# Head pairs stacked on 64x64 array tiles, the second dense product moved to the slot tiles, half of the expert weights loaded late

## The chip, the cores and the metric

The kernel runs on one core of one Trainium2 chip. The metric is the device time of one execution in microseconds; shown times are medians of several runs. A core has five engines with their own instruction queues: PE (matmuls; its weight loads are listed apart as PEld), DVE, ACT, POOL and SP. SP only issues transfers here; POOL computes and also issues the transfers that cast or that gather and scatter rows. Every transfer runs on the core's 16 DMA engines. SBUF is the on-chip memory, PSUM holds matmul results until DVE or ACT has read them (eight banks of 2 KB for each of 128 partitions).

## The reference

Attention with normalised q and k, then a mixture of experts with one expert for each token beside a dense layer that every token passes.

```python
# q, k, v: (8, 12, 448, 64) float32; x below: 3584 tokens of 768
def rmsnorm(x, g):
    return x / np.sqrt(np.mean(x * x, axis=-1, keepdims=True) + 1e-06) * g
scores = (1 / np.sqrt(64)) * np.matmul(rmsnorm(q, g_q), rmsnorm(k, g_k).transpose(0, 1, 3, 2))
attn = softmax(scores)                     # over the last axis
x = np.matmul(attn, v)                     # heads side by side: 12 * 64 = 768
y_dense = np.maximum(x @ w1_dense, 0.0) @ w2_dense          # 768 -> 512 -> 768
expert_idx = np.argmax(x @ w_gate, axis=1)                  # 8 experts
gate_w = softmax(x @ w_gate)[arange, expert_idx]
for e in range(8):                                          # 768 -> 512 -> 768
    y_moe[mask_e] = gate_w[mask_e] * (np.maximum(x[mask_e] @ w1[e], 0.0) @ w2[e])
out = y_dense + y_moe
```

## The kernel before

**Attention** goes in 48 steps `t`, one for two heads (a pair), six for a batch. The 448 positions of a head are spread as 112 partitions of `JJ` = 4. q and k come in groups `g` of two pairs (L141, on SP), v as bf16 (L145, on POOL). `squares` (L161 on POOL, L162 on DVE) and L167/L168 on ACT give 1/rms as `r`; `normalise` multiplies on DVE (L177); `transposes` brings q and k to 64 rows a head (L186) and copies them out on DVE (L191 with the gains, L193). `scores(t, j)` multiplies 64 rows of k by q for both heads (L202), each head in its half of the rows, and ACT takes the exp of 112 x 896 values (L204). `attend(t, hh)` multiplies the exps by v with a column of ones (L215, 16 matmuls), and DVE divides by the sum (L219, L221). `xtrans` transposes the result (L228, copied by ACT, L230); after six pairs `route(b)` makes the logits of a batch (L239), takes the best expert into `oh`, and SP writes x and the gate into a table `records` in HBM, one row for each token (L260 to L264).

The dense layer of the batch before runs in pieces between these: `dense1` (L273, relu on ACT, L276) and `dense2` (L284, copied by ACT and DVE, L289 and L291); SP writes the 768 results into the token's record (L293). The 16 expert weight blocks, 768 KB each in bf16, are cast on the way by transfers that POOL issues every 2.5 steps (L329) into `we`, which holds all experts.

In attention the order on PE, POOL and SP is the program's order, written by hand: in step `t` come scores of `t + 1`, transposes of `t + 2`, squares of `t + 4`, normalise of `t + 3`, attend of `t`, and pieces of the dense layer. DVE and ACT are ordered by the compiler. Four PSUM buffers (`wkp`) serve transposes, attend, dense and logits; two pairs of banks serve the scores.

**The slot table** (L357 to L442) follows when all batches are routed: for each token its place among the tokens of its expert, then a one-hot `sel` (L410) and `val` (L416), and 32 matmuls (L422) that give for each slot the record's `row` and the output row `dest`. A slot tile is 128 slots of one expert; there are 35.

**The slot tiles**: POOL gathers 128 records (L449), PE transposes x (L460), multiplies by the expert's w1 (L469, relu and gate on ACT, L474), transposes (L479, copied by ACT, L481) and multiplies by w2 (L487); DVE adds the dense result from the record (L493) and POOL scatters the rows to the output (L495).

## Time and profile before

| | |
|---|---|
| median of 3 runs | 518.86 us (514.01 to 518.98) |
| the profiled execution: time, span | 519.15 us, 517.3 us |
| busy: PE, DVE, ACT, POOL | 399.3, 326.6, 274.8, 205.3 us |
| granted PE clock, mean | 0.92 |
| HBM read, written | 83.16 MB, 31.20 MB |
| first scores | 27.4 us |
| last attend ends | 335.3 us |
| first gather is issued | 373.9 us |
| first transpose of a slot tile, last w2 matmul | 379.1 us, 510.1 us |

The profile page lists one profiled execution. In rows of groups, `out<-in` names the tiles, x is the count, then come busy us and mean ns of one instruction, then the idle time ahead and what ended it. Windows give the busy us of each engine in a stretch of the span, the granted clock of PE (1.00 is full), the share of time that the 16 DMA engines were busy, and GB/s. Timeline rows begin with start and length in us; an x above 1 means that many instructions merged into one row, and a length of matmuls reaches to the end of the last one's pipeline, so that the pace is read from start to start.

### The profile page before, as it was taken

Reading aid. Unit: us, or ns where it says so; the run is one execution under the profiler, and the core shown is the slowest. Engines: PE = TensorE matmul, PEld = TensorE weight load, DVE = VectorE, ACT = ScalarE, POOL = GpSimd, SP = SyncE. Lnnn points to the kernel's source line nnn. Section 1 sums busy time; section 2 is a strip of 40 time slices with the busy share of each in tenths; the row PEclk is TensorE's granted clock in tenths of the full one; section 3 lists DMA queues with packets and bytes.
Section 4 is the critical chain, followed back from the end, with each engine's and each line's share of the span. In section 5 each row is a group of like instructions: output and inputs, shape, how many; then the busy total and the mean of one; then the engine's idle time right before and its main releaser. Section 6 shows DMA issues by size and latency. Waiting matters only on the chain.

```text
span 517.3 us, 10774 instructions
## 1 busy us (share of the span) xinstructions
PE 399.3 (77%) x4010; PEld 232.7 (45%) x4010; DVE 326.6 (63%) x761; ACT 274.8 (53%) x431; POOL 205.3 (40%) x223
## 2 busy tenths in 40 slices
PE   0189888769688887788977979980249889899894
PEld 0046645435344454454543545650215555556552
DVE  3796999868568779588786975427603434444442
ACT  0077887648567756767855978730003333333331
POOL 6674354453426327128136130000023555556542
PEclk9999999979888989979977999996559999999998
DMA  8999679997798599959879441251063878888860
GB/s 142 237 218 175 151 154 159 192 256 96 176 269 137 137 271 142 198 133 239 187 134 248 107 144 30 81 152 46 1 241 122 278 253 266 286 283 266 294 259 2
DMA packets 66017, 92.62 MB, mean 179 GB/s; under 512 B 8749, under 2 KB 56109, under 8 KB 65968
## 3 DMA queue, kind: packets, MB, share of 16 engines
q0 software_dynamic: 31568, 52.48, 45.4%
q1 hardware_dynamic: 34400, 39.46, 27.6%
q8 instruction: 33, 0.54, 0.4%
q14 instruction: 16, 0.13, 0.1%
HBM read 83.16 MB, written 31.20 MB: 221 GB/s over the span
## 4 chain that ended last, share of the span: by engine, by line
PE 30%; DMA 27%; DVE 20%; ACT 7%; issue 6%; POOL 6%; SPq 2%; POOLq 0%; DVEq 0%; ACTq 0%
DMA xq<-in_q_dram 9%; DMA xg<-records,row 9%; DMA xk<-in_k_dram 8%; DVE y L177 7%; PE he L469 5%; PE av L215 5%; DVE ssq L162 5%; PE ps L202 5%; PE yp L487 4%; ACT ex L204 4%; POOL sq L161 4%; PE ff L273 4%; PE ff L284 2%; DVE xa L221 2%; PE tr L186 2%
## 5 line engine op out<-in xcount | busy, mean ns | idle before, releaser
L204 ACT ACTIVATE ex<-ps 112x896 bf16<-112x896 f32 x192 | 173.8, 921 | 54.3 <-PE ps L202 52.7
L161 POOL TENSOR_TENSOR sq<-xq 112x512 f32<-112x512 f32 x48 | 52.1, 1085 | 141.8 <-DMA xq<-in_q_dram 118.8
L162 DVE TENSOR_REDUCE ssq<-sq 112x8 f32<-112x512 f32 x96 | 64.0, 672 | 42.9 <-POOL sq L161 42.9
L202 PE MATMUL ps<-y 64*112 64x448 bf16 x384 | 84.1, 435 | 2.5 <-DVE y L193 1.3
L215 PE MATMUL av<-va,ex 112*128 112x65 bf16 x1536 | 71.2, 202 | 17.7 <-DVE xa L221 16.0
L215 PEld LDWEIGHTS <-ex 112*128 112x128 bf16 x1536 | 59.3, 103 | 40.9 <-DVE xa L221 21.3
L284 PE MATMUL ff<-wd,hT 128*112 128x384 bf16 x256 | 60.4, 347 | 10.8 <-DVE xa L221 10.8
L449 POOL DMA_INDIRECT xg<-records,row x35 | 33.9, 967 | 81.1 <-DVE dest L442 70.4
L186 PE MATMUL tr<-ident,y 112*128 112x112 bf16 x384 | 39.2, 232 | 29.0 <-DVE y L177 24.2
L161 POOL TENSOR_TENSOR sq<-xk 112x512 f32<-112x512 f32 x48 | 51.3, 1070 | 19.1 <-DVE ssq L162 9.8
L495 POOL DMA_INDIRECT out_dram<-ys,dest x35 | 35.6, 1018 | 58.6 <-DVE ys L493 58.6
L474 ACT ACTIVATE hs<-he,xg 128x512 bf16<-128x512 f32 x35 | 24.0, 687 | 65.6 <-DMA xg<-records,row 36.3
L469 PE MATMUL he<-we,xT 128*128 x210 | 53.5, 393 | 3.0 <-issue 1.5
L462 DVE COPY xT<-xp 128x768 bf16<-128x768 bf16 x35 | 19.5, 557 | 57.5 <-PE xp L460 57.5
L202 PEld LDWEIGHTS <-y 64*112 64x112 bf16 x384 | 26.2, 131 | 61.6 <-issue 56.0
L273 PE MATMUL ff<-xT,wd 128*128 128x448 bf16 x192 | 52.1, 373 | 2.1 <-DVE xa L221 2.1
L487 PE MATMUL yp<-we,heT 128*128 x280 | 51.2, 326 | 0.8 <-DVE ys L493 0.8
L493 DVE TENSOR_TENSOR ys<-yp,xg 128x768 f32<-128x768 f32 x35 | 33.5, 957 | 28.0 <-PE yp L487 28.0
L481 ACT COPY heT<-hp 128x512 bf16<-128x512 bf16 x35 | 20.5, 586 | 49.1 <-PE hp L479 49.1
L186 PEld LDWEIGHTS <-y 112*128 112x128 bf16 x384 | 22.9, 104 | 51.0 <-DVE y L177 25.3
L177 DVE TENSOR_TENSOR y<-xq,r 112x512 bf16<-112x512 f32 x48 | 45.0, 937 | 0.9 <-ACT r L168 0.9
L221 DVE TENSOR_TENSOR xa<-av,inv 128x256 bf16<-128x256 f32 x96 | 40.1, 418 | 1.4
(98 smaller groups left out, 473.3 us busy)
## 6 DMA issues: line engine op xcount, KB each, us to landing
we<-in_moe_w_dram POOLq DMA_DIRECT2D x16, 768.0 KB, 8.4
records<-ys SPq DMA_DIRECT2D x32, 336.0 KB, 3.3
xq<-in_q_dram SPq DMA_DIRECT2D x23, 448.0 KB, 6.7
xk<-in_k_dram SPq DMA_DIRECT2D x23, 448.0 KB, 7.0
vr<-in_v_dram POOLq DMA_DIRECT2D x24, 224.0 KB, 5.9
records<-xa SPq DMA_DIRECT2D x8, 576.0 KB, 7.4
wd<-in_moe_w_dense_dram POOLq DMA_DIRECT2D x2, 768.0 KB, 19.4
records<-xa SPq DMA_DIRECT2D x8, 96.0 KB, 7.0
```

The source lines that it names most:

```text
L161: nc.gpsimd.tensor_mul(sq, x, x)
L162: nc.vector.tensor_reduce(ssqs[g][:, n, 2 * i * JJ:(2 * i + 2) * JJ], sq.rearrange("p h (j d) -> p (h j) d", d=D), AX.X, ALU.add)
L177: nc.vector.tensor_mul(y.rearrange("p j h d -> p h j d"), x.rearrange("p h (j d) -> p h j d", d=D), rs[g][:, n, 2 * i * JJ:(2 * i + 2) * J ...
L186: nc.tensor.transpose(ps[:, j * SC:(j + 1) * SC], xn[name, t][:, j].rearrange("p h d -> p (h d)"), ident[:SC, :SC])
L202: nc.tensor.matmul(ps[:, hh, :S], qkT["k", t][d0:d0 + D, j * SC:(j + 1) * SC], qkT["q", t][d0:d0 + D, :], start=True, stop=True)
L204: nc.scalar.activation(exs[t][:, j], ps[:, :, :S], AF.Exp, scale=scale)
L215: nc.tensor.matmul(av[:, mi], exs[t][:, j, hh, QC[mi]:QC[mi] + P], vas[t // GP][:, 2 * (t % GP) + hh, j, :De], start=(j == 0), stop=(j == ...
L221: nc.vector.tensor_mul(xnats[b][:, :, h * D:(h + 1) * D], av[:, :, :D], inv.to_broadcast([P, 4, D]))
L273: nc.tensor.matmul(ffs[0], wd1[:, kk, ff * P:(ff + 1) * P], xTs[b][:, kk], start=(kk == 0), stop=(kk == KD - 1))
L284: nc.tensor.matmul(ffs[0], hTs[b][:, ff, j * SC:(j + 1) * SC], wd2[:, ff, dd * Dm // 2:(dd + 1) * Dm // 2], start=(ff == 0), stop=(ff == F ...
L469: nc.tensor.matmul(he, xTs[t][:, kk], we[:, bass.ds(eregs[t], 1), 0, kk * F:(kk + 1) * F] .rearrange("p o f -> p (o f)"), start=(kk == 0), ...
L487: nc.tensor.matmul(yp[:, dd, :HD], heTs[t][:, ff], we[:, bass.ds(eregs[t], 1), 1, ff * Dm + dd * HD:ff * Dm + (dd + 1) * HD] .rearrange("p ...
```

## The change

- Attention goes in 24 groups `g` of four heads. The 448 positions are spread as 64 partitions of `J` = 7, and two heads lie one above the other in the 128 partitions, `(r p)`. `scores(g, j)` is four matmuls of 64 rows by 64 columns, one for each quarter of the array, and one exp of 128 x 896; there are 7 of them in a group. `attend` multiplies 64 rows at a time, for the two stacked heads in turn: 112 matmuls a group; its two PSUM accumulators are filled over four calls.
- k is divided on POOL (q stays on DVE), v is copied on POOL, transposed k is copied out on ACT, transposed x on DVE.
- In a group, scores come in each of seven slots `i`, attend in the even ones, and full-array work (transposes, logits, ranks, dense) in the odd ones.
- Exps live in 14 buffers that are the last part of `we` (the space of experts 6 and 7 and the end of 5).
- Loads of q and k are called for group `g + 5` at the start of group `g`, in three buffers as before; one load fills 128 partitions with pieces of 1792 bytes instead of 1024.
- The dense layer's first product has tokens as rows; its relu, 512 values in bf16, is written to the record instead of the 768 results (a record has 704 instead of 1216 words). The second product is done in the slot tiles: each gathers the hidden values, transposes them (`hdTs`) and accumulates them with `wd2` into the same PSUM as the expert's product. DVE and ACT copy half of the sum each.
- Places within an expert and `sel` are made batch by batch (`ranks`); the slot table gives two values a slot instead of three, and every expert has at least one slot tile, so that tile `t` reads no expert above `t`.
- Of the 16 expert blocks eight are issued during attention, every 2.6 groups, and eight (experts 4 to 7) at the end of POOL's order in attention, ahead of the gathers.
- The gains are loaded from ACT's queue; constants are made after the first loads are issued.

```diff
-    JJ = 4
-    SC = S // JJ
+    J = 7
...
+    LATE, WPACE = 8, 2.6
...
+        xflat = we.rearrange("p e a f -> p (e a f)")[:, -NX * 2 * S:]
+        exr = [xflat[:, i * 2 * S:(i + 1) * 2 * S].rearrange("p (h s) -> p h s", h=2)
+               for i in range(NX)]
...
+                "(i r) (p j) d -> (r p) i (j d)", r=2, j=J)
...
+            nc.gpsimd.tensor_copy(vabs[g % 3][:, :, :, :D],
+                                  xin["v", g].rearrange("p h (j d) -> p h j d", d=D))
...
+        def squares(g, name):
+            x = xin[name, g]
+            ssq = sb.tile([P, 2, J], F32, tag="ssq" + name)
+            for hh in range(2):
+                sq = sb.tile([P, J * D], F32, tag="sq", bufs=3)
+                nc.gpsimd.tensor_mul(sq, x[:, hh], x[:, hh])
+                nc.vector.tensor_reduce(ssq[:, hh], sq.rearrange("p (j d) -> p j d", d=D), AX.X,
+                                        ALU.add)
+            r = sb.tile([P, 2, J], F32, tag="r" + name)
+            nc.scalar.activation(r, ssq, AF.Ln, bias=eps_t, scale=1.0 / D)
+            nc.scalar.activation(r, r, AF.Exp, scale=-0.5)
+            rs[name, g] = r
+
+        def normalise(g, name):
+            eng = nc.vector if name == "q" else nc.gpsimd
+            y = sb.tile([P, J, 2, D], BF16, tag="xn" + name, bufs=1)
+            for hh in range(2):
+                eng.tensor_mul(y[:, :, hh], xin[name, g][:, hh].rearrange("p (j d) -> p j d", d=D),
+                               rs[name, g][:, hh].unsqueeze(2).to_broadcast([P, J, D]))
+            xn[name, g] = y
...
             if name == "q":
-                nc.vector.tensor_scalar(y, ps, gqk, None, op0=ALU.mult)
+                nc.vector.tensor_scalar(o, i, gqk, None, op0=ALU.mult)
             else:
-                nc.vector.tensor_copy(y, ps)
-            qkT[name, t] = y
-
-        def scores(t, j):
-            if j == 0:
-                exs[t] = sb.tile([SC, JJ, 2, S], BF16, tag="ex", name="ex")
-            ps = scp.tile([SC, 2, 512], F32, tag="sc")
+                nc.scalar.copy(o, i)
...
+        def scores(g, j):
+
+            x = exr[(g * J + j) % NX]
+            exs[g, j] = x
+            qT, kT = qkT["q", g], qkT["k", g]
+            ps = scp.tile([P, 2, 512], F32, tag="sc", name="sc")
             for hh in range(2):
-                d0 = hh * D
-                nc.tensor.matmul(ps[:, hh, :S], qkT["k", t][d0:d0 + D, j * SC:(j + 1) * SC],
-                                 qkT["q", t][d0:d0 + D, :], start=True, stop=True)
-            nc.scalar.activation(exs[t][:, j], ps[:, :, :S], AF.Exp, scale=scale)
-
-        def attend(t, hh):
-
-            b, pr = divmod(t, NPR)
-            if pr == 0 and hh == 0:
-                xnats[b] = sb.tile([P, 4, Dm], BF16, tag="xa", name="xa")
+                rows = slice(hh * D, (hh + 1) * D)
+                for r in range(GP):
+                    nc.tensor.matmul(ps[r * D:(r + 1) * D, hh, :S], kT[rows, r, j],
+                                     qT[rows, r].rearrange("p j s -> p (j s)"),
+                                     start=True, stop=True)
+            nc.scalar.activation(x, ps[:, :, :S], AF.Exp, scale=scale)
...
+            va = vabs[g % 3]
+            if m == 0:
+                for r in range(GP):
+                    avs[r] = wkp.tile([P, 4, De], F32, tag="wk", name="av")
+            for j in range(J):
+                for r in range(GP):
+                    rows = slice(r * D, (r + 1) * D)
+                    nc.tensor.matmul(avs[r][:, m], exs[g, j][rows, hh, QC[m]:QC[m] + P],
+                                     va[rows, hh, j, :De], start=(j == 0), stop=(j == J - 1))
+            if m < 3:
+                return
+            for r in range(GP):
+                inv = sb.tile([P, 4, 1], F32, tag="inv")
+                nc.vector.reciprocal(inv, avs[r][:, :, D:])
+                h = 4 * gb + 2 * hh + r
+                nc.vector.tensor_mul(xas[b][:, :, h * D:(h + 1) * D], avs[r][:, :, :D],
+                                     inv.to_broadcast([P, 4, D]))
...
+            nc.vector.tensor_copy(xTs[b][:, gb * GP:(gb + 1) * GP], ps)
...
+        def ranks(b):
+
+            rk = wkp.tile([P, 5, E], F32, tag="wk", name="rk")
+            mm = [(rk[:, :4], tri, oh[:, b])]
+            mm += [(rk[:, i:4], ones, oh[:, b, :4 - i]) for i in range(1, 4)]
+            mm += [(rk[:, 4:], ones, oh[:, b, m:m + 1]) for m in range(4)]
...
+            nc.vector.tensor_tensor(sel[:, b], iop.unsqueeze(1).to_broadcast([P, 4, P]),
+                                    lo[:, b].unsqueeze(2).to_broadcast([P, 4, P]), ALU.is_equal)
...
+        def dense(n):
+            b, n = divmod(n, 4 * KD)
+            m, kk = divmod(n, KD)
+            if kk == 0:
+                ff[0] = wkp.tile([P, F], F32, tag="wk", name="ff")
+            nc.tensor.matmul(ff[0], xTs[b][:, kk, QC[m]:QC[m] + P], wd1[:, kk],
+                             start=(kk == 0), stop=(kk == KD - 1))
+            if kk == KD - 1:
+                hd = sb.tile([P, F], BF16, tag="hd", bufs=1)
+                nc.scalar.activation(hd, ff[0], AF.Relu)
+                r0 = b * S + m * P
+                n = P if m < 3 else D
+                nc.sync.dma_start(rec[r0:r0 + n, XH:GO], hd[P - n:].bitcast(F32))
...
+                for g in range(3):
+                    for name in "qk":
+                        squares(g, name)
+                        normalise(g, name)
+                        if g < 2:
+                            transposes(g, name)
+                    if g < 2:
+                        values(g)
+                    load(g + 3)
+                load_v(1)
...
+                for g in range(NG + 1):
+                    b, gb = divmod(g, NB)
+                    if g % 2 == 0:
+                        load_v(g // 2 + 2)
+                    if g > 0:
+                        load(g + 5)
...
+                    for i in range(J):
+                        if g + 1 < NG:
+                            scores(g + 1, i)
+                        if g < NG and i % 2 == 0:
+                            for m in range(2):
+                                attend(g, i // 4, i % 4 + m)
+                        if i == 1:
+                            if g > 0:
+                                xtrans(g - 1)
+                            if g + 2 < NG:
+                                transposes(g + 2, "q")
+                        if i == 3 and gb == 0 and g > 0:
+                            logits(b - 1)
+                        elif i == 5 and g + 2 < NG:
+                            transposes(g + 2, "k")
+                        if i == 5 and gb == 0 and g > 0:
+                            ranks(b - 1)
+
+                        if i % 2 and i > 1 and g >= NB and (gb > 0 or i == 5):
+                            for _ in range(5):
+                                if nd < (b - 1) * 4 * KD + 4 * KD:
+                                    dense(nd)
+                                    nd += 1
+                        if g + 3 < NG:
+                            if i % 4 == 0:
+                                squares(g + 3, "qk"[i // 4])
+                            if i % 4 == 2:
+                                normalise(g + 3, "qk"[i // 4])
+                        if i == 4 and g + 2 < NG:
+                            values(g + 2)
+                while nd < 4 * KD * B:
+                    dense(nd)
+                    nd += 1
+                while nw < len(wjobs):
+                    nc.gpsimd.dma_start(*wjobs[nw])
+                    nw += 1
+
+        run({PE, POOL, SP})
...
+            hp = ps1.tile([P, FT, P], BF16, tag="tr")
+            for i in range(FT):
+                nc.tensor.transpose(hp[:, i], xb[:, Dm + i * P:Dm + (i + 1) * P], ident)
+            hdTs[t] = sb.tile([P, FT, P], BF16, tag="hdT", name="hdT")
+            nc.vector.tensor_copy(hdTs[t], hp)
...
-            eregs[t] = nc.tensor.value_load(tei[:, t:t + 1], min_val=0, max_val=E - 1)
+            eregs[t] = nc.tensor.value_load(tei[:, t:t + 1], min_val=0, max_val=min(t, E - 1))
...
+                    nc.tensor.matmul(yp[:, dd, :HD], hdTs[t][:, i],
+                                     wd2[:, i, dd * HD:(dd + 1) * HD],
+                                     start=(i == 0), stop=False)
...
-            nc.vector.tensor_add(ys, yp[:, :, :HD],
-                                 xgs[t][:, XH:GO].rearrange("p (a d) -> p a d", a=2))
+            nc.vector.tensor_copy(ys[:, 0], yp[:, 0, :HD])
+            nc.scalar.copy(ys[:, 1], yp[:, 1, :HD])
```

## The prediction

> **What bounds the kernel now.** I read the stages first (windows of the span), then the DMA queues, then single stretches of the timeline, last the chain that ended last. Busy times of a window stand in the order PE, weight load, DVE, ACT, POOL, then granted clock, DMA share, GB/s.
>
> ```profile
> 50.00:75.00 25.00, 22.79 (x306) 13.79 (x304) 23.25 (x60) 21.57 (x34) 9.27 (x9) 1.00 0.69 151
> 125.00:150.00 25.00, 19.41 (x230) 11.45 (x231) 16.17 (x46) 15.61 (x25) 5.56 (x6) 0.89 0.94 192
> 312.00:335.00 23.00, 23.00 (x286) 13.53 (x283) 11.28 (x31) 19.61 (x30) 0.00 (x0) 1.00 0.14 39
> 379.10:517.30 138.20, 118.14 (x840) 68.69 (x840) 53.02 (x70) 44.54 (x70) 65.54 (x66) 0.94 0.69 232
> ```
>
> In the middle of attention no engine is full, but the DMA share is 0.94 and the clock sags. Counted by the exps (four to a step), the same windows for L204 alone give the pace:
>
> ```profile
> 50.00:75.00 25.00, 17.75 (x20) 1.00 0.69 151
> 125.00:150.00 25.00, 12.28 (x15) 0.89 0.94 192
> 300.00:325.00 25.00, 14.73 (x17) 1.00 0.21 63
> ```
>
> 20 exps in 25 us are 5.0 us a step; from 100 to 300 us all windows together hold 119, so 6.7 us a step, 13.4 us for two steps (one group of four heads). The waits and queues say why:
>
> ```profile
> POOL sq L161 <- DMA xq<-in_q_dram: 118.8, 13, 12.1
> q0 software_dynamic: 31568, 52.48, 45.4%
> q1 hardware_dynamic: 34400, 39.46, 27.6%
> ```
>
> 27.6% of 517.3 is 143 us of full DMA for 39.46 MB: 3.6 us/MB. q0 has 235 us; the tile stage, all q0, takes 0.69 of its 138 us and a little before, so 98; the other 137 us are the v and weight casts, 19.4 MB written: 7.1 us/MB, 5.5 us for a 768 KB expert job. Attention thus carries 280 us of transfers, and waits for them. PE's own pace is read where no loads are left:
>
> ```profile
> 311.06 0.40 PE L202 MATMUL ps<-y 64*112 64x448 bf16 x2
> 311.39 0.56 PEld L215 LDWEIGHTS <-ex 112*128 112x128 bf16 x16 [0.20 <-issue]
> 311.88 0.13 PEld L273 LDWEIGHTS <-wd 128*128 128x128 bf16 x2
> 311.92 0.54 PE L273 MATMUL ff<-xT,wd 128*128 128x448 bf16 x2
> 312.39 0.13 PEld L202 LDWEIGHTS <-y 64*112 64x112 bf16 x2 [0.37 <-issue]
> ```
>
> From start to start: the score pair takes 0.33 us, less than twice the 0.19 that one dense matmul of 448 columns is given, so its two 64-row halves run together and in the rest PE starts nothing; some 0.09 is lost ahead of it too: 0.42 a call. Sixteen attend matmuls take 0.49: 31 ns each. The slot tiles run at PE's pace except for gathers:
>
> ```profile
> 452.29 1.46 PE L469 MATMUL he<-we,xT 128*128 x6
> 453.58 0.50 PE L460 MATMUL xp<-ident,xg 128*128 128x128 bf16 x6
> 453.92 1.46 PE L487 MATMUL yp<-we,heT 128*128 x8
> 455.21 0.39 PE L479 MATMUL hp<-ident,hs 128*128 128x128 bf16 x4
> 455.44 1.46 PE L469 MATMUL he<-we,xT 128*128 x6
> ```
>
> Starts differ by 1.29, 0.34, 1.29, 0.23: 3.15 us a tile. Between the last attend (335.3) and the first gather issue (373.94) lie 38.6 us, a third of it three rows:
>
> ```profile
> 360.83 4.34 DVE sel L410
> 365.16 3.58 DVE val L416
> 368.78 3.00 PE slp L422 x32
> ```
>
> **The slot tiles: +38 us, the surest term.** The second dense product moves here: 8 more matmuls of 384 columns (1.29) and 4 more transposes (0.23) make 3.15 + 1.52 = 4.67 us a tile, 163 for 35. I add 6 us from first landing to steady running (two transposes and a gemm1 that took 2.72 at half clock) and the 7 us from the last L487 to the end: 176 against 138. A gather now brings 2.8 KB a slot instead of 4.9, so a tile moves 0.75 MB instead of 1.02 in a longer time, and I cost the wait for gathers at nothing; ACT and DVE, with the halves of ys, stay under 2 us a tile.
>
> **Transfers in attention: 280 to 210 us.** Eight expert jobs leave (44), and hidden activations are stored as 3.7 MB instead of 11 MB of products (26). Over a stage of some 260 us this is a share of 0.8. Loads are also called two groups ahead instead of one, and the SP queue is no longer held by the L293 stores. I cost the wait for loads at nothing; what hides it is that slack. Without it a 7 us load per group would show in part.
>
> **One group of four heads, engine by engine.** PE: 7 score calls of four 64x64 matmuls. The pair's second matmul costs nearly nothing now (lower bound 0.42 a call); upper bounds are 0.61 if two go together and 0.99 if none do. Both halves of the pair already overlap, so I take 0.47: 3.3 us. Attend: 112 matmuls of 64 rows instead of 64 of 112 rows. Bounds are 25 ns (19 logits matmuls took 0.47) and 31; at 28 it is 3.1 us, where it was 2.0. Transposes 0.7, xtrans 0.45, first dense product 8.3 at 0.215 = 1.8, logits and ranks 0.3. PE: 9.65. The second dense product, 1.9 us a group, is gone from here.
>
> The row says that a load of 112 columns shows 123 ns against 98 for 128 columns, so the narrower load is the slower one. The Trainium skill's "TensorEngine Tiling (Array Packing)", Restrictions, says that column tiling switches fast weight load off; by "TensorE: Matmul & The Clock Gate", LDWEIGHTS, 64 columns would take 53 ns. Four of them in a row, unhidden, would add 0.16 a call, an estimate of 27 us in all and a time near 532; by the pair's row it is 0.05.
>
> DVE: four square sums 0.672 x 448/512 (2.4), q divided (1.6 by L177), q transposes out (0.9), four inv and xa (2.4), x transposes out, taken from ACT (0.8), logits and ranks (1.1): 9.1; it was 11.6. ACT: seven exps at 0.92 (6.5), k transposes out, taken from DVE (1.1), relu (0.9), r (1.1): 9.5. POOL: squares 3.8, k division 1.9 by the same two-input row, v copy between 0.6 (DVE's L152) and 1.9 (L161 scaled), taken as 1.2, issues 0.8: 7.7. So three engines lie within 6%.
>
> PE's order then waits for PSUM. Two av accumulators are held across three slots, a dense accumulator across two, and four wk buffers serve all. Where av of the last half is still being read, xt and tr follow one another through one buffer (a 0.8 us copy plus DVE's queue), and a new ff waits for the relu. What queues behind is everything on PE, scores first, then ACT's exps. Bounds: 0 (before kept 93 to 100% of its fullest engine) to 2.6 us; I take 1.6. A group takes 11.3 us where it took 13.4. All this is at full clock; the granted clock was 0.86 to 0.97 from 100 to 300 us, where PE waited most, and 1.00 from 50 to 75 and after 300, so I expect 1.00. At 0.9 the 9.65 would be 10.7, which is 23 us in all and lies within the rivals' span.
>
> **Attention's end.** First scores need two whole groups, q and k, with k divided on POOL: 32 us where it was 27.4, then 6 for seven exps: 38. Three groups without dense 9.5 each, nineteen at 11.3, the last two 10 and 7: 298 instead of 335.3, so -37.
>
> **From there to the gather: 38.6 to 18 us.** The dense product and ys stores end (10 us), scans and positions are done per batch, sel too. Left: transposes, logits, ranks 7; counts and hi 2.5; tl and two val products of 1120 elements, 2 to 4 by L413's 1.32; slp 3.0; row and issue 1.6.
>
> **Late weights: +6 us.** Three jobs are free about 19 us ahead of attention's end, two follow when the last group but one is attended, three more only at its end, because exps lie in their place. At 5.5 each they drain near 26 us after it, and the gathers, in the same queue, are issued at 18. No row shows a gather behind weights. Bounds: nothing, landing 5.1 us after issue as now, to all eight after attention's end, 44 us and 2 more. I take landing at 29, so 6 us over. By the Trainium skill's "DMA: Bandwidth & Descriptors", section "Two DMAs through the same engine are not ordered", descriptors of one queue of one DMA engine start in order, which would give the same 29; no row here shows it.
>
> **Sum.** 298 + 29 + 176 = 503, against 517.3. The profiled execution took 519.15 with 1.85 around its span; the median is 518.86. So **505**; beside the median that is 0.3 us less, within its spread (514.01 to 518.98). Each us on a group is 22 us; no gain is left at 11.9 us a group.
>
> **Rivals.** (1) PSUM handover decides: PE's order stalls 2.6 us a group or more. For it: DVE, ACT and PE are almost equally full and four buffers carry long tenants; against: the 312 to 335 window, full PE. From 11.9 us a group it is slower; at 12.5, 505 + 26 = 531. (2) The engines overlap as well as in the 50 to 75 window, 93%: 10.4 us a group, 485. Against it: the longer tenants. (3) Weights hold the gathers whole: landing at 46 instead of 29, 522. For it: POOL waits in order, and a first job that waits for exps delays all behind it.
>
> **How the numbers follow.** Forecast 0.55, rival 1 0.20, rival 2 0.17, rival 3 0.08. A measurement here tells about 1% from no change. The forecast's own range is 492 to 518; the range, 482 to 530, leaves out the ends of rivals 1 and 2. Faster: 0.50 of the forecast, all of rival 2 and a little of 3; the same: the rest of the forecast and most of 3.
>
> **What would show it.** Seven exps every 11.3 us; DMA share near 0.8 in attention and the POOL wait for xq gone; score calls start to start under 0.5 us; tiles at 4.67; first gather issue 18 us after the last attend and landing some 11 later. It is wrong if groups take over 12 us, if score calls take 0.6 or more, or if gathers land over 40 us after attention.

## The result, and the profile after

The changed kernel takes 558.42 us (median of 4 runs, 557.07 to 560.32) where the kernel before takes 518.25 (4 runs on the same chip): a ratio of 1.079, 95% interval 1.072 to 1.086. Slower by 8%; the prediction was 505. The profiled execution took 559.05, its span 557.4. By stages:

| stage | before | predicted | after |
|---|---|---|---|
| first exp starts (predicted: first scores) | 28.1 | 32 | 25.9 |
| a group of four heads (exps 3 to 21) | 13.45 | 11.3 | 14.38 |
| last attend ends | 335.3 | 298 | 349.5 |
| from there to the first gather issue | 38.7 | 18 | 27.4 |
| from the issue to the first xg transpose | 5.2 | 11 | 3.9 |
| from there to the end | 138.2 | 176 | 176.6 |

By spans the miss is 54.4 us (557.4 against 503), and 51.5 of it lie in attention. What is lost from there to the first gather (9.4 us) is mostly made up by the first transpose behind it (7.1). The windows of after show the three stages (busy time in the order PE, weight load, DVE, ACT, POOL, then granted clock, DMA share, GB/s):

```profile
25.90:349.50 323.60, 243.22 (x4240) 139.50 (x4236) 189.07 (x485) 196.93 (x312) 157.88 (x178) 0.78 0.58 131
349.50:376.00 26.50, 13.31 (x96) 8.07 (x95) 9.71 (x41) 3.81 (x7) 1.57 (x2) 0.70 0.66 141
384.00:557.40 173.40, 165.81 (x1240) 101.97 (x1238) 49.38 (x103) 58.08 (x105) 64.76 (x65) 0.97 0.39 130
```

In attention no engine is full, PE is busy for 75% of the time, the DMA share is 0.58 where 0.8 was predicted, and the granted clock is 0.78. So the shares point neither to transfers nor to the work of any one engine. The instructions themselves came out cheaper than predicted, as PE's timeline shows where the clock is full, and the slot tiles came out as predicted:

```profile
195.04 0.38 PE L226 MATMUL sc<-y 64*64 64x448 bf16 x4
195.36 0.62 PE L244 MATMUL av<-va,we 64*128 64x65 bf16 x28
195.90 0.38 PE L226 MATMUL sc<-y 64*64 64x448 bf16 x4
...
440.99 1.46 PE L507 MATMUL he<-we,xT 128*128 x6
...
445.67 1.46 PE L507 MATMUL he<-we,xT 128*128 x6
```

From start to start, four 64x64 score matmuls take 0.32 us, and 28 attend matmuls 0.54 us, 19 ns each. A tile is 445.67 - 440.99 = 4.68 us.

What PE, POOL and VectorE wait for in attention is in the lists of waits from 60 to 310 us (who <- for what: us in all, times, longest):

```profile
PE av L244 <- DVE xa L252: 31.8, 16, 3.8
PE tr L206 <- DVE xT L263: 10.1, 11, 2.4
PE rk L302 <- DVE oh L284: 6.4, 5, 2.4
PE ff L329 <- ACT y L214: 5.5, 7, 0.9
...
POOL y L198 <- PE tr L206: 100.2, 12, 9.9
...
DVE ssq L187 <- POOL sq L186: 42.0, 27, 6.9
```

PE waits for VectorE to empty the av accumulators (xa), VectorE stands at POOL's squares, and POOL stands at PE's transposes of k: a ring. One turn of it, from the timeline (start, duration, engine; in brackets the idle time before and who ended it):

```profile
130.09 1.83 POOL L198 TENSOR_TENSOR y<-xk,r 128x448 bf16<-128x448 f32 x2 [7.17 <-PE tr L206]
131.87 0.81 POOL L172 DMA_DIRECT2D xv<-in_v_dram  x1
132.71 1.83 POOL L186 TENSOR_TENSOR sq<-xq 128x448 f32<-128x448 f32 x2
...
133.68 0.62 DVE L187 TENSOR_REDUCE ssq<-sq 128x7 f32<-128x448 f32 x1 [6.82 <-POOL sq L186]
134.57 0.62 DVE L187 TENSOR_REDUCE ssq<-sq 128x7 f32<-128x448 f32 x1 [0.26 <-POOL sq L186]
135.10 0.24 DVE L250 RECIPROCAL inv<-av 128x4 f32<-128x4 f32 x2
...
135.79 0.95 PE L244 MATMUL av<-va,we 64*128 64x65 bf16 x27 [2.42 <-DVE xa L252]
```

The tile of the divided k (xn) has one buffer, so POOL may not divide the next k until PE has transposed the last one; everything behind it in POOL's order, a v load and the next squares, is late by those 7 us. VectorE's order has the square sums (L187) ahead of inv and xa (L250, L252), so it holds the av accumulators meanwhile, and PE stands for 2.42 us. What happens to the clock is in five windows of 3.41 us around that gap:

```profile
131.49:134.90 3.41, 1.89 (x40) 0.90 (x38) 0.95 (x2) 1.14 (x2) 3.39 (x5) 1.00 0.56 139
134.90:138.31 3.41, 2.44 (x39) 1.80 (x40) 2.26 (x8) 2.37 (x6) 2.28 (x3) 0.50 1.16 245
138.31:141.73 3.42, 2.79 (x44) 1.73 (x44) 2.42 (x6) 0.97 (x2) 0.00 (x0) 0.50 0.18 63
141.73:145.14 3.41, 3.41 (x39) 1.37 (x37) 0.79 (x4) 2.07 (x3) 0.00 (x0) 0.50 0.11 38
145.14:148.55 3.41, 3.34 (x73) 1.85 (x68) 0.00 (x0) 3.20 (x5) 2.25 (x3) 1.00 0.01 2
```

The clock is 1.00 or 0.50, and in this trace it changes only at the edges of such windows. PE is busy for 0.55 of the first one, and the clock falls. It is busy for 0.71 and 0.82 of the next two, at half clock, and only after a window that it fills does the clock return: a gap of 2.42 us is followed by 10.2 us at half clock.

The same cut through the profiles of all sixteen kernels of the table below, from 60 to 310 us, shows what goes ahead of a change. At full clock, all 92 windows in which PE was busy for at most half were followed by half clock, and none of the 323 with 0.78 or more; of the 351 between, 90 were. At half clock, 133 of 139 windows with 0.95 or more were followed by full clock, 55 of 90 from 0.85 to 0.95, and 1 of 158 below that. So in these traces the clock follows how much PE was busy, and once it has fallen, short waits are enough to keep it down.

The clock's record begins with its first return to full, at 39.3 us here. Ahead of that the views read 1.00, but a score call takes 0.59 us, as it does at 0.50 later, instead of 0.38; these windows are counted as half clock above.

At the end of attention, the chain that ended last goes through writes of hd, whose tile has one buffer:

```profile
336.49 5.38 DMA records<-hd
...
342.59 7.24 DMA records<-hd
...
350.55 5.19 DMA records<-hd
...
356.47 5.31 DMA records<-hd
...
366.02 1.70 DMA records<-hd
...
370.89 4.02 PE slp L447 x32
```

Alone a write takes 1.7 us; beside the late expert weights, 5 to 7.

### The profile page after: what moved, and what is told of

It is laid out like the page before. It is cut to its first block, busy times and chain, and to the rows that moved or that the text cites. A ratio compares the mean times of both kernels' runs of the same rounds, so it can differ in the third digit from the quotient of the medians.

```text
span 557.4 us, 14089 instructions
## 1 busy us (share of the span) xinstructions
PE 429.4 (77%) x5628; PEld 254.7 (46%) x5628; DVE 262.0 (47%) x723; ACT 263.9 (47%) x434; POOL 250.4 (45%) x285
## 4 chain that ended last, share of the span: by engine, by line
issue 29%; PE 23%; POOL 21%; DVE 15%; DMA 8%; ACT 2%; POOLq 1%; ACTq 0%; DVEq 0%
POOL sq L186 8%; POOL xg L485 6%; PE av L244 6%; PE sc L226 6%; PE ff L329 5%; DMA records<-hd 5%; PE tr L206 4%; POOL y L198 3%; POOL out_dram L539 2%; DVE ssq L187 2%; PE xt L260 2%; DVE xa L252 2%; DVE xT L263 1%; DMA gk<-in_g_k_dram 1%; DVE tj L315 1%
## 5 line engine op out<-in xcount | busy, mean ns | idle before, releaser
L229 ACT ACTIVATE we<-sc 128x896 bf16<-128x896 f32 x168 | 150.1, 915 | 65.9 <-PE sc L226 65.1
L198 POOL TENSOR_TENSOR y<-xk,r 128x448 bf16<-128x448 f32 x48 | 44.8, 954 | 135.5 <-PE tr L206 109.9
L244 PE MATMUL av<-va,we 64*128 64x65 bf16 x2688 | 75.5, 208 | 38.6 <-DVE xa L252 32.3
L244 PEld LDWEIGHTS <-we 64*128 64x128 bf16 x2688 | 59.2, 105 | 67.0 <-DVE xa L252 35.3
L187 DVE TENSOR_REDUCE ssq<-sq 128x7 f32<-128x448 f32 x96 | 57.5, 614 | 55.7 <-POOL sq L186 55.2
L226 PE MATMUL sc<-y 64*64 64x448 bf16 x672 | 76.3, 446 | 8.7 <-ACT we L229 6.6
L329 PE MATMUL ff<-wd,xT 128*128 128x512 bf16 x192 | 68.3, 501 | 6.9 <-ACT y L214 5.5
L507 PE MATMUL he<-we,xT 128*128 (+1 forms) x210 | 53.6, 394 | 0.2 <-issue 0.2
L526 PE MATMUL yp<-wd,hdT 128*128 128x384 bf16 x280 | 51.2, 326 | 1.1 <-ACT ys L538 1.1
L531 PE MATMUL yp<-we,heT 128*128 (+1 forms) x280 | 51.2, 326 | 0.0
L186 POOL TENSOR_TENSOR sq<-xk 128x448 f32<-128x448 f32 x48 | 44.0, 930 | 11.2 <-DVE ssq L187 11.2
## 6 DMA issues: line engine op xcount, KB each, us to landing
we<-in_moe_w_dram POOLq DMA_DIRECT2D x16, 768.0 KB, 10.2
```

Source lines behind the costliest of these rows:

```text
L186: nc.gpsimd.tensor_mul(sq, x[:, hh], x[:, hh])
L187: nc.vector.tensor_reduce(ssq[:, hh], sq.rearrange("p (j d) -> p j d", d=D), AX.X, ALU.add)
L198: eng.tensor_mul(y[:, :, hh], xin[name, g][:, hh].rearrange("p (j d) -> p j d", d=D), rs[name, g][:, hh].unsqueeze(2).to_broadcast([P, J, D]))
L226: nc.tensor.matmul(ps[r * D:(r + 1) * D, hh, :S], kT[rows, r, j], qT[rows, r].rearrange("p j s -> p (j s)"), start=True, stop=True)
L229: nc.scalar.activation(x, ps[:, :, :S], AF.Exp, scale=scale)
L244: nc.tensor.matmul(avs[r][:, m], exs[g, j][rows, hh, QC[m]:QC[m] + P], va[rows, hh, j, :De], start=(j == 0), stop=(j == J - 1))
```

## The experiments

Each is the changed kernel with the edit shown. One run each, with a profile, except e14_hd3_late5 and e12 (medians of 4) and e14_late5 (of 10); the kernel before took 514.97 us beside e1 to e4, and 518.68 to 520.76 beside the others. PE's busy and idle time a group is its time from 60 to 310 us, divided by the groups in it (250 us over the group's time); clock and gaps are of that stretch, a gap being the time between matmul records. In e5, e6 and e12 the record of the clock begins at 67.6, 69.2 and 71.2 us only, so that their clock is some 0.02 lower than the views, and the table, give it.

| run | time | group | PE busy | PE idle | clock | gaps over 2 us | last attend | to the gather |
|---|---|---|---|---|---|---|---|---|
| kernel before | 518.25 | 13.45 | 11.2 | 2.3 | 0.92 | 4 | 335.3 | 38.7 |
| changed kernel | 558.42 | 14.38 | 10.8 | 3.6 | 0.73 | 13 | 349.5 | 27.4 |
| e1_xn2 | 550.80 | 13.43 | 9.9 | 3.6 | 0.81 | 9 | 334.9 | 34.6 |
| e2_kdve | 532.60 | 13.01 | 9.6 | 3.4 | 0.88 | 9 | 324.8 | 27.0 |
| e4_dveorder | 548.28 | 13.25 | 9.7 | 3.6 | 0.82 | 8 | 339.6 | 27.7 |
| e5_wk6 | 553.83 | 13.39 | 10.2 | 3.1 | 0.82 | 5 | 345.5 | 28.2 |
| e9_kdve_hd2 | 531.37 | 13.35 | 10.2 | 3.2 | 0.84 | 10 | 325.3 | 24.1 |
| e6_kdve_wk6_hd2 | 519.99 | 11.78 | 9.2 | 2.5 | 0.90 | 0 | 314.4 | 24.6 |
| e11_e6_dveorder | 517.26 | 11.49 | 9.0 | 2.5 | 0.90 | 1 | 311.1 | 24.3 |
| e14_late5 | 517.10 | 11.44 | 9.0 | 2.4 | 0.91 | 0 | 309.9 | 24.3 |
| e14_hd3_late5 | 510.44 | 11.27 | 8.9 | 2.4 | 0.92 | 0 | 307.1 | 23.5 |
| e7_dup | 584.54 | 15.52 | 11.7 | 3.8 | 0.82 | 10 | 374.2 | 27.5 |
| e8_hd2 | 550.62 | 14.41 | 10.6 | 3.8 | 0.75 | 14 | 346.5 | 24.2 |
| e3_hd4 | 558.12 | 14.37 | 10.5 | 3.8 | 0.72 | 14 | 344.9 | 30.2 |
| e10_late | 571.41 | 14.27 | 10.6 | 3.7 | 0.75 | 15 | 343.5 | 20.6 |
| e12_paced | 553.76 | 11.58 | 9.1 | 2.4 | 0.90 | 0 | 313.6 | 19.4 |

**The ring through POOL.** e1 gives the divided k two buffers (and, for room, opens the pool of the slot table only in the second stage); e2 takes the division from POOL to VectorE; e4 leaves POOL as it is and has VectorE follow the written order too.

```
e1:  y = sb.tile([P, J, 2, D], BF16, tag="xn" + name, bufs=1)    ->  bufs=2
e2:  eng = nc.vector if name == "q" else nc.gpsimd               ->  eng = nc.vector
e4:  run({PE, POOL, SP})                                         ->  run({PE, DVE, POOL, SP})
```

> Two buffers instead of one for divided q and for divided k (the slot table's pool is moved behind attention to make room). Theory A: k's division on POOL waits for PE's transposes of the group before, because it has one buffer (106.8 us of waits between 60 and 330 us); so POOL's squares come late, DVE's square sums stand ahead of the av evacuation in DVE's order, and PE waits for PSUM. Then POOL's wait for tr falls under 30 us, PE's wait for xa falls by more than half, the group period falls from 13.9 to 12 us or less, and the total to 505 to 525. Rival B, PSUM handover alone (four wk buffers with long tenants): POOL's wait falls, but PE's stays, the period stays over 13 and the total within 545 to 562.

> k is divided on DVE again, all else as changed. If the place of the division is what costs (POOL's order blocked by it, theory A; or POOL and DVE slowing each other), POOL no longer waits for tr, squares run ahead, the period falls to about 12.5 in spite of 1.3 us more DVE work a group: total 520 to 535. If DVE's own fullness is what costs, the period rises: 565 or more. Rival B: no change, 550 to 562.

> DVE's order in attention is the program's too, instead of the compiler's; nothing else is changed. Theory D: the compiler put square sums, which wait for POOL, ahead of the av evacuation that PE waits for. In the program's order the evacuation stands ahead of the square sums of k of the same half, so PE's wait for xa (32 us) falls to under 10, the period to 12.5 or less, total 515 to 530. If the loop through the single buffer of k (theory A) is what sets the pace, the order changes where the wait shows, not its size: 545 to 565.

All three loosen the ring, and in all three the group falls to 13.0 to 13.4 us, no further. The last attend comes 14.6, 24.7 and 9.9 us earlier. e1 gives 7.2 us of it back in the next stage, because the pool that it moves makes the slot table wait for the hd writes. Against the expectations: e2's time is in its range, with a longer group than 12.5; in e1 the waits for tr and xa fall as theory A had it, but the group (over 13) and the time (545 to 562) are its rival's; e4's time is that of the loop through k's buffer (545 to 565). The waits of e1 (its lines stand one lower) show the wait of PE gone and the next one in its place:

```profile
PE tr L205 <- DVE xT L262: 16.9, 12, 3.6
PE rk L301 <- DVE oh L283: 10.0, 6, 2.7
PE ff L328 <- ACT y L213: 8.1, 6, 1.9
PE av L243 <- DVE xa L251: 7.1, 11, 3.5
...
POOL va L177 <- PE av L243: 100.8, 17, 10.1
...
DVE ssq L186 <- POOL sq L185: 35.3, 30, 7.8
```

The wait for xa falls from 31.8 to 7.1 us, but PE's idle time a group stays at 3.6: the waits for a handover tile take over. POOL still stands for 100.8 us, now at the v copy behind attend, and VectorE at its squares for 35.3 us instead of 42.0, so the ring is looser and not gone. What fell is PE's busy time for the same work, 10.8 to 9.9 us, as the clock rose from 0.73 to 0.81.

**The handover in PSUM.** e5 gives the shared pool six tiles instead of four and the scores one instead of two, which is all the room there is; e9 has k on VectorE and two hd tiles, e6 these two and e5's split.

```
e5:  a_sc bufs=2 -> bufs=1;  a_wk bufs=4 -> bufs=6
e9:  eng = nc.vector;  hd = sb.tile([P, F], BF16, tag="hd", bufs=1) -> bufs=2
e6:  e5 and e9
```

> Two of the eight PSUM banks go from the scores (one score tile instead of two) to the pool of transposes, attend, logits, ranks and dense (six buffers instead of four). Nothing else is changed. Theory B (PSUM handover: PE waits for a free one of four buffers): PE's waits for DVE's xa and xT, 42 us between 60 and 310 us, fall under 15, the clock rises, the group period falls from 14.4 to 12 or less, total 500 to 525. Theory A (POOL's late squares set the pace): the period stays over 13.4, total 540 to 560. Against both: with one score tile each slot's scores wait for the exp of the slot before, which costs something if slots are shorter than 1.3 us.

> The same PSUM split, with k divided on DVE and two hd buffers. If A and B both cost and are separate, the period falls below that of either alone (13.0 with k on DVE): 10.5 to 11.5, the end from attend to gather to 20 us, total 475 to 495. If they are the same loop seen twice: 12 to 13, total 505 to 525.

> k divided on VectorE and two hd tiles, PSUM left as in the change (two score tiles, four handover tiles): the combination before it, less the PSUM part. Theory (k's division and the PSUM handover are two loops that must both be opened): the 26 us of k's division and the 8 of hd add, some 524 to 528 us, with a group at 12.6 to 13.0 us. Rival (the single score tile and the six handover tiles brought nothing, the combination's gain was k and hd): 521 us or less, a group at 12.0 or less.

Alone the six tiles bring 4.6 us (558.4 to 553.8), which fits the expectation of the ring (540 to 560). But the total hides two things. In the middle, from group 3 to 21, a group is 0.99 us shorter, 17.8 us in all; ahead of it 11.6 us are lost, as group 3 starts at 63.6 us instead of 52.0. There, without the dense layer, a group takes 12 to 13.5 us with one score tile and 7.6 to 9.5 with two. Its chain goes back and forth between the scores into the one tile and the exp:

```profile
39.83 0.93 ACT we L229
...
40.80 0.61 PE sc L226 x4
...
41.43 0.93 ACT we L229
```

PE is busy for only 0.63 of the time from 26 to 63.6 us, and the first return to full clock comes at 67.6 us instead of 39.3. In all runs of the changed kernel with one score tile it comes between 58 and 72 us, in those with two between 27 and 43.

Beside e9 the six tiles bring 11.4 us (531.4 to 520.0) and 1.57 us a group, with a like loss ahead (group 3 at 65.1 instead of 53.8). And k with hd, without them, stop at 531, above the 524 to 528 expected, so that hd's second tile adds almost nothing to e2. That e2 and e9, which are alike in attention but for hd, have groups of 13.01 and 13.35 us shows how far such a number varies.

So two loops hold attention, each of them undone alone shortens the group, and what they bring adds up, as far as single runs tell: 0.99 and 1.37 us a group alone, 2.60 together. The same holds for the times (4.6, 25.8 and 7.8 us for the six tiles, k and hd alone, 38.4 together). One loop seen twice would have given no more together than alone. e6's group of 11.78 lies just above the 10.5 to 11.5 expected of two loops. Its time of 520 misses their 475 to 495 and lies in the range of one loop (505 to 525), but 13 us of it go ahead of group 3, and the gap to the gather stays at 24.6. The waits of e9, then of e6:

```profile
PE tr L206 <- DVE xT L263: 21.1, 12, 3.6
PE rk L302 <- DVE oh L284: 11.9, 6, 2.6
```

```profile
PE sc L226 <- ACT we L229: 46.6, 91, 1.2
PE rk L302 <- DVE oh L284: 6.0, 4, 1.9
```

In e6 the tall waits are gone but for the one at rk. PE now waits for the one score tile, 91 times for half a microsecond: seven rounds of a score call (0.41), an exp (0.93) and the 0.06 between them make 9.8 us of the 11.8.

**Is PE's work the bound, or the clock?** e7 issues every score matmul twice, which computes the same.

```
+ for _ in range(2):
      nc.tensor.matmul(ps[r * D:(r + 1) * D, hh, :S], ...)
```

> Each score matmul is issued twice, the second overwriting the first with the same values: 28 more matmuls a group, about 1.4 us at full clock. Theory E: half of the lost time is the granted clock (0.75 in attention), which falls because PE is idle and would rise if it were kept at work: clock 0.9 or more, period under 14.4, total under 558. Without E the clock stays under 0.8 and the period rises by 1.4 to 1.9 us: 590 to 600.

At 0.32 us a call the extra work is 2.2 us a group at full clock, 3.1 at the 0.73 granted before. The group grows by 1.1, while the clock rises from 0.73 to 0.82. That lies between the two expectations (0.9 and under 558 us, or under 0.8 and 590 to 600). So with more work PE did get a faster clock, and part of the added work went into time that was lost; but 10 gaps over 2 us are left, and keeping PE busy with idle work does not pay: the whole is 26 us slower.

**The writes of hd and the late weights.** e8 and e3 give hd two and four tiles (e3 moves the slot table's pool as e1 does). e10 issues the eight late weights on POOL behind the first four gathers; e12 issues one behind each of the first eight gathers of the tile loop, on top of e11.

```
e8:   hd ... bufs=1 -> bufs=2        e3:  bufs=1 -> bufs=4
e10:  - while nw < len(wjobs): nc.gpsimd.dma_start(*wjobs[nw]); nw += 1
      + for job in wjobs[-LATE:]: nc.gpsimd.dma_start(*job)          (behind gather(3))
e12:  + if t < LATE: nc.gpsimd.dma_start(*wjobs[t - LATE])           (behind gather(t + 4))
```

> Two hd buffers instead of one, all else as changed (the earlier run with four also moved the slot table's pool, whose first instruction then waited for the last records). Theory C: from the end of attend to the first gather 27 us fall to 18 to 21, attention itself is as before; total 546 to 553. Without C no change, 555 to 560.

> Four buffers instead of one for the hidden values hd (slot table's pool moved as in the other run). Theory C: each relu waits until the record of the one before has landed, 26 us of ACT waits around attention's end, where late weights stretch those writes from 1.7 to 7 us. Then attention's end to the first gather falls from 27 to under 18 us, and the last three groups shorten: total 530 to 545, period in the middle unchanged at 13.9. Theory A alone would leave the end as it is for other reasons: 550 to 560.

> The changed kernel, but the eight late expert weights are issued on POOL after the first four gathers instead of ahead of them. Theory (the casts stretch the writes of hd beside them): the hd writes at the end of attention return to about 1.7 us, last attend some 3 us earlier, last attend to first gather 27.4 -> about 21, and the tiles keep 4.7 us, as the first late expert is needed some 16 tiles on: 558 -> 547 to 551 us. Rival (the casts only move): the gathers that follow now wait behind them, the tile stage grows from 176 to 185 or more, and the time stays at 553 to 560.

> k divided on VectorE, six handover tiles with one score tile, two hd tiles, VectorE in written order (517.3 us so far), and the eight late expert weights issued one behind each of the first eight gathers of the tile loop. Theory: hd's writes are no longer stretched, so the last attend comes 3 to 6 us earlier and the first gather some 20 us after it instead of 24.3; a gather is issued four tiles (18.7 us) ahead, which hides one 5 us cast in front of it, so the tiles keep 4.67 us: 506 to 511 us, faster than the kernel before by 1.5 to 2.5%. Rival (any cast in front of a gather shows): the first eight tiles take 1 to 3 us more each, 515 to 530 us.

e8: 3.0 us at the last attend, 3.2 behind it and the rest in the slot tiles, 7.8 in all. Its time is in the range expected, its gap of 24.2 is not (18 to 21): one write of 8.0 us is left on the chain. e3, expected at 530 to 545, gains 4.6 us at the last attend and loses 2.8 behind it, to the moved pool. e10 shows what the weights cost where they are: without them on the way, the hd writes on the chain take 1.7 us, the last attend comes 6.0 us earlier and the gather follows after 20.6 instead of 27.4. But as a whole it is slower than even the rival had it, since from the first transposes to the end it takes 201.6 us instead of 176.6. Its timeline:

```profile
369.02 6.46 POOL L549 DMA_DIRECT2D we<-in_moe_w_dram  x8
379.46 1.02 POOL L482 DMA_INDIRECT xg<-records,row  x1 [3.97 <-DMA we<-in_moe_w_dram]
...
406.54 0.82 PE L491 MATMUL xp<-ident,xg 128*128 128x128 bf16 x6 [20.97 <-DMA xg<-records,row]
```

The gather issued at 379.46, behind eight weights, is used at 406.5. e12 (1.069 of the kernel before, 1.057 to 1.081) spreads the weights out, and its gather does come 19.4 us after the last attend; but from the first transposes to the end it takes 218.6 us, slower than its rival had it too. Its waits from 336 to 425 us:

```profile
PE he L504 <- DMA we<-in_moe_w_dram: 19.7, 3, 12.9
PE yp L528 <- DMA we<-in_moe_w_dram: 9.1, 1, 9.1
PE xp L491 <- DMA xg<-records,row: 6.7, 2, 6.0
```

My expectation held that the first late expert is needed some 16 tiles on. The program cannot know that: the expert of a tile is read from a register, which gemm1 bounds by `min(t, E - 1)`, so tile 5 has to wait for expert 5, whose first load is issued only two turns of the loop before. Ahead of the tiles is the cheapest of the three places tried.

**Put together.** e11 is e6 with VectorE in written order. e14_late5 is e11 with five late weights instead of eight; e14_hd3_late5 has three hd tiles as well, and for room two of sq.

```
e11:            run({PE, POOL, SP}) -> run({PE, DVE, POOL, SP})
e14_late5:      LATE, WPACE = 8, 2.6 -> 5, 2.0
e14_hd3_late5:  e14_late5;  hd bufs=3;  sq bufs=3 -> bufs=2
```

> k divided on VectorE, six handover tiles with one score tile, two hd tiles, and VectorE's instructions also in written order. Theory (in the changed kernel the planner's VectorE order cost 10 us only because VectorE stood at POOL's late squares; with k off POOL they are no longer late): no more than 3 us from the same kernel without the order, 517 to 523 us. Rival (the planner's order costs by itself): another 6 to 10 us less, 510 to 514 us.

> As the kernel with k on VectorE, six handover tiles, two hd tiles and VectorE in written order (517.3 us), with five late expert weights instead of eight: the other three are loaded in attention, where the DMA share is 0.66. Theory (the casts at the end stretch hd's writes): the 8.2 us write on the chain before the slot table shrinks to 2 to 5 us, last attend to first gather 24.3 to 19 to 21, attention as before: 512 to 514 us. Rival (three more casts slow attention's loads): the group goes from 11.5 to 11.8 or more and takes the gain back, 517 to 521 us.

> The same, with three hd tiles (and two of sq instead of three, for room). Theory (what is left on that chain is the wait for a free hd tile): a write stands on the chain no longer, last attend to first gather about 16 to 18 us, 508 to 512 us. Rival (two sq tiles make POOL's squares late again, or the writes of xa take their place): no faster than with two hd tiles.

e11 bears out that VectorE's order mattered through the ring: it brought 10 us in e4 and 2.7 here, 1.13 and 0.29 us a group. In both, the first exp starts some 6 us later (32.3 and 32.5 us instead of 25.9 and 26.7). e14_late5 refutes its theory: 517.1 us (0.996 of before, 0.992 to 1.000), the group no slower, and the gap still 24.3. The last four weights still start as late as before, at 305.43 and 310.29 behind the last exps (306.61 and 311.46 in e11), and the write on the chain still takes 8.0 us. e14_hd3_late5 takes 510.44 us, 0.985 of the kernel before (0.973 to 0.996): faster than both, though by only 1.5% against the kernel before. That is in the range expected, but not for the reason expected: it has a shorter group and a last attend 2.8 us earlier, while its gap is 23.5, not 16 to 18; its chain still holds

```profile
311.87 2.59 PE ff L329 x6
...
315.15 8.73 DMA records<-hd
...
324.64 4.02 PE slp L447 x32
```

So the write is not just queued behind too few hd tiles; it is slow. Taking it off the chain, for instance with room for the last four hd tiles, was not tried.

## Why the prediction was wrong, step by step

**Right.** The slot tiles: 176 predicted, 176.6 measured, 4.68 us a tile against 4.67. The start came earlier than predicted (first exp at 25.9, first scores predicted at 32). Transfers relieved: POOL's wait for xq is gone, at a DMA share of 0.58 rather than 0.8. Engines: each does less a group than predicted (POOL 6.9 us for 7.7, VectorE 8.5 for 9.1, ACT 8.3 for 9.5, by their busy time from 60 to 310). PE's own work is about 10.8 x 0.73 = 7.9 us at full clock, not 9.65 (an estimate: the same product gives 7.6 to 8.5 in the other kernels, which do the same work). The score call at 0.32 lies below the 0.47 taken, so the 0.16 of unhidden weight loads that the prediction weighed does not show (a load lists 103 ns, but is hidden), and attend, at 19 ns, lies below its lower bound of 25.

**Wrong: "at 28 it is 3.1 us ... so I expect 1.00", the clock.** The prediction read the clock from stretches that had full clock and set it to 1.00, with 0.9 as the bad case. It was 0.73: 10.8 - 7.9 = 2.9 us a group by that estimate (2.3 to 3.2 by its spread), the largest term of the miss. The prediction had the evidence (the sag lay "where PE waited most") and did not use it. By the windows the clock goes by how much PE was busy in the 3.41 us before, so a long wait of any cause can bring it down, and the changed kernel has 13 gaps over 2 us where the kernel before has 4.

**Wrong in size: "I take 1.6", the waits.** PE's idle time is 3.6 us a group, above the bound of 2.6. The three terms close the sum: 7.9 + 2.9 + 3.6 = 14.4, where 9.65 + 1.6 was 11.3.

**Missed: POOL's place in the order.** k's division was costed at 1.9 us of POOL's busy time, a price that held (0.95 each, two a group). But the step asked only what POOL would do, not what POOL would wait for: one xn tile, freed by a transpose in a later slot, and squares queued behind it. By e1, with a second tile, the one tile cost 14.6 us up to the last attend; by e2 the division's whole place on POOL cost 24.7. The rule that a wait's price includes what is queued behind it was applied to PE alone.

**Rival 1 named the mechanism but not the price.** PE's order did stall by more than 2.6 us a group, and part of it at PSUM, as e5, e6 and e9 show. At 12.5 us a group and 531 it fell short for two reasons: it left out the ring, and it priced stalls at their own length. From the changed kernel to e14_hd3_late5 the group falls by 3.1 us, of which the idle time is 1.2 and PE's faster clock 1.9.

**"Late weights: +6", right in sum by luck, wrong in place.** Gathers were predicted to land 29 us after the last attend, held by weights; the transposes started after 31.3, and the gathers waited for nothing: 3.9 us from issue. The weights held the hd writes instead, and these held the slot table: 27.4 us instead of 18, of which e10 gives 6.8 back. Rival 3, weights holding gathers, shows only in e10, where gathers follow right behind the weights.

**Still open.** Between half and 0.78 busy the windows don't tell which one loses the clock, so the pattern of gaps alone does not give 0.82 or 0.88 (e5 has five gaps over 2 us, e2 nine and the higher clock). No run changed the clock alone. And in every kernel with one score tile group 3 starts 11 to 15 us later than in the changed kernel; nothing was tried against that.

## What to carry to other kernels

When work moves to an engine in fixed order, ask what the moved instruction waits for and who stands behind it, above all where its output has one buffer; its busy time is the smaller part of its price. Price a stall of PE at more than its length: in this kernel the slower clock cost, by the estimate above, almost as much as the gaps themselves (2.9 and 3.6 us a group). And read an undo stage by stage: e5's 4.6 us were 17.8 gained in the middle and 11.6 lost at the start, and the total alone would have called that loop harmless.

## What the runs showed of the hardware

**Half clock from short gaps.** The clock was 1.00 or 0.50, nothing between, it changed at the edges of windows of 3.41 us, and a gap of 2.42 us was followed by 10.2 us at 0.50. The Trainium skill, "TensorE: Matmul & The Clock Gate", "What's actually happening", says that the ratio takes two values and is judged in free-running windows of 3.4 us; the two values, and the five windows above, agree with that. Its rule of thumb in "HAM oscillation — how this bites in real kernels", no idle gaps above some 3.4 us, is too mild here: from 60 to 310 us the changed kernel's clock fell 14 times, and only one of its gaps was over 3.4 us.

**Small VectorE instructions in step with POOL.** On 128x4 values, these take 0.16 to 0.17 us when POOL is idle. Beside POOL's squares:

```profile
203.95 1.82 POOL L186 TENSOR_TENSOR sq<-xq 128x448 f32<-128x448 f32 x2
205.73 0.93 POOL L186 TENSOR_TENSOR sq<-xk 128x448 f32<-128x448 f32 x1
...
204.05 0.86 DVE L314 TENSOR_SCALAR ri<-ri 128x4 int32<-128x4 int32 x1
204.94 0.86 DVE L315 CAST tj<-ri 128x4 f32<-128x4 int32 x1
205.83 0.85 DVE L316 SCALAR_TENSOR_TENSOR lo<-tj,rf 128x4 bf16<-128x4 f32 x1
```

Each takes 0.86 us and ends as a square of POOL's ends: one small instruction for each of POOL's. The Trainium skill, "SBUF — State Buffer", "SBUF: two separate sides", tells of a port pair that VectorE and GpSimd lock for a whole instruction; these rows fit it. The ranks of a batch, costed with the logits at 1.1 us a group (3.3 a batch), took 5.2 us on the chain in this place.

**Row tiles at 19 ns.** At full clock, 28 attend matmuls of 64 rows and 65 columns, in alternating halves of the array, took 19 ns each, where the 19 logits matmuls of the kernel before, with 128 rows and 8 columns, took 25 each.
